# Row blocks of 128 and a remainder, and one transfer per gather, in the expert part of a fused kernel

## The chip, the cores and the metric

One Trainium2 chip; the kernel runs on one core, in one launch. Its engines are TensorE (PE: matmuls, and beside it PEld, the loading of the stationary operand), VectorE (DVE), ScalarE (ACT), GpSimd (POOL) and SyncE (SP, which here only issues transfers). Sixteen DMA engines move data between DRAM and the on-chip memory. The metric is the device time of a launch in microseconds; smaller is better. All data are 4 bytes wide.

## The reference, cut to what matters

A linear-attention recurrence, a dense layer pair, and a layer of eight experts of which every token uses one. The change touches only the last:

```python
N, D, E, F = (3072, 384, 8, 1024)
...
logits = x @ w_gate
e_idx = np.argmax(logits, axis=1)
...
gate_w = probs[np.arange(N), e_idx]
eom = 1.0 / (1.0 + np.exp(-(x @ w_output_gate)))
out = np.zeros((N, D), dtype=np.float32)
for e in range(E):
    mask = e_idx == e
    ...
    h = np.maximum(x[mask] @ w1[e], 0.0)
    ye = h @ w2[e]
    out[mask] = gate_w[mask, None] * eom[mask, e, None] * ye
```

So each token's row of 384 numbers goes through two matrices of one expert, is scaled, and is written to the token's place.

## The kernel before, in words

The first 560 us are attention and the dense pair, for eight blocks of 384 tokens. As each block is done, the rows of its tokens are scattered into a DRAM table `rows`, sorted by expert: a row has 386 numbers (384 values, the scale, the token's number), 1544 bytes. Each expert has its own region of the table, of which the first 512 rows (`CAPS[0]`) are filled beforehand with blank rows whose token number is invalid.

Then come the experts, the fullest first. The list `CAPS` says how many rows each place in that order gets: 512, 456, 432, 424, 408, 384, 384, 372. They are worked as nine segments, numbered 0 to 8: the first expert is two segments of 256 rows, every other one is a segment of its own, so that segment 2 has 456 rows and segment 8, the last, has 372. `segs` holds, for each, the expert, the first row, the number of rows and a tuple with the rows of its token blocks (lines 773 to 777):

```python
mb = -(-n // 128)
segs.append((i, 0, n, (128,) * 3 + (n - 384,) if 384 < n <= 448 else (n // mb,) * mb))
```

That makes 4 blocks of 114 for segment 2, three blocks of 128 and one of 48, 40 or 24 for segments 3 to 5, three of 128 for segments 6 and 7, and three of 124 for segment 8.

For one segment the work is:

- `gather` (L792): SP issues a transfer of the segment's rows from `rows` to the tile `xs`, with a block's rows on as many partitions (L805); where the last block is shorter, a second transfer fetches it (L807).
- `turn_x` (L810): for each of three column groups `kc`, PE transposes the blocks (L815), ACT copies the result to `xe` (L816), DVE forms the low part (L817) and, once, the token numbers `ids` (L820, and L822 for a shorter last block).
- `first` (L830): for each of eight column groups `f`, nine matmuls with all the segment's rows as the moving operand (L839), then ACT and DVE make `hh`.
- `second` (L851): for each block and each `f`, matmuls with the block's columns of `hh` as the stationary operand and 384 columns moving (L867): three for each block, or two where a short last block has both parts of its rows side by side (`packed`, L789).
- `finish` (L870): the blocks are scaled by ACT or DVE (L883, L881, L879), and for each POOL issues an indirect transfer that scatters its rows to `out` (L885).

In this part of the program the order on every engine is that of the code. In segment q, at step f = 2, SP gets the gather of segment q + 1; at f = 4, 5 and 6 PE gets its transposes. Beside that, at steps set by `plan`, SP fetches the next expert's weights in seven pieces (`fetch`, L749 and L754, 512 and 384 KB each) into a few buffers, and ACT with DVE or POOL splits them (`split`, L768, L769). SP works its list in order, so a gather stands behind the fetches before it and ahead of those after it.

At the end, the last three `f` of segment 8 are worked block by block, so that each block's scatter can start while the next is still being multiplied.

Of the kernel before, what the change touches and what calls it, by code (L numbers as in the profile page):

```python
# [18 lines left out]
B, H, S, D = 4, 8, 768, 48  # L19
DM = H * D  # L20
FF = 2048
NT = B * S
E = 8
FE = 1024
CH = 64
TB = 384
NC = TB // CH
NBLK = NT // TB
NP = H // 2
# [20 lines left out]
def consts():  # L50
    c = np.zeros((128, 384), np.float32)
    p = np.arange(128)
    c[:, 0:128] = np.eye(128)
    c[:, 128:192] = (p[:, None] % CH) <= np.arange(CH)[None, :]
    c[:, 192:320] = p[:, None] < p[None, :]
    c[:, 320:328] = E - np.arange(E)
    c[:, 328:336] = np.arange(E)
    c[:, 360:368] = CAPS
    c[:, 368:376] = NT * (p[:, None] < np.arange(E)[None, :])
    c[:, 336:360] = np.arange(NT // 128)[None, :] * 128 + p[:, None]  # L60
    return c
# [3 lines left out]
def tile_kernel(ctx, tc, aps, outs):  # L65
    nc = tc.nc
    pe, act, dve, pool, sp = nc.tensor, nc.scalar, nc.vector, nc.gpsimd, nc.sync
# [23 lines left out]
    rows = dp.tile([E * NT, ROW], F32, name="rows")  # L91
# [358 lines left out]
    sent = {}  # L450

    def apart(key, i):
        # every token has its own row
        for b in sent.setdefault(key, []):
            tc.declare_no_dep(i.ins, b.ins, reason="no two tokens share a row")
        sent[key].append(i)

    def route_send(j):
        oh, ps = rs.pop(j)
        r = rt.pop(j)[0]  # L460
        pr = rp.tile([128, NA, E], F32, name="pr2")
        si = rp.tile([128, NA], I32, name="si")
        dve.tensor_tensor(out=pr, in0=ps[:, 0:NA * E].rearrange("p (a e) -> p a e", e=E), in1=oh, op=ALU.mult)
        with nc.allow_low_precision(reason="whole numbers below 2**24"):
            dve.tensor_reduce(out=si, in_=pr, axis=AX.X, op=ALU.add)
        for a in range(NA):
            apart("rows", pool.indirect_dma_start(
                out=rows, out_offset=bass.IndirectOffsetOnAxis(ap=si[:, a:a + 1], axis=0),
                in_=r[:, a], in_offset=None, bounds_check=E * NT - 1, oob_is_err=False))
        for a in range(NA):  # L470
            dve.tensor_tensor(out=cum, in0=cum, in1=oh[:, a], op=ALU.add)
# [21 lines left out]
    ex = {}  # L493
# [233 lines left out]
    for j in range(NBLK):  # L727
        last = j == NBLK - 1
# [4 lines left out]
        if last:  # L733
# [34 lines left out]
                act.copy(hi, t)  # L768
                (dve, pool)[i % 2].tensor_tensor(out=lo, in0=t, in1=hi.bitcast(F32), op=ALU.subtract)  # L769

            # segments: expert place, first row, rows, rows of its token blocks;
            # a last block of up to 64 rows has both parts of its rows side by side in one stationary operand
            segs = [(0, 0, EARLY, (128,) * 2), (0, EARLY, CAPS[0] - EARLY, (128,) * 2)]
            for i, n in enumerate(CAPS):
                if i:
                    mb = -(-n // 128)
                    segs.append((i, 0, n, (128,) * 3 + (n - 384,) if 384 < n <= 448 else (n // mb,) * mb))
            HH = [mh.tile([128, 2 * CAPS[1]], F32R, name=f"hh{i}") for i in range(3)]
            for t in HH:
                pool.tensor_copy(out=t[:, 384:448], in_=cst[:, 376:377].to_broadcast([128, 64]))  # L780
# [2 lines left out]
            def blocks(q):  # L783
                at = 0
                for m, mr in enumerate(segs[q][3]):
                    yield m, mr, slice(at, at + mr)
                    at += mr

            def packed(q, m):  # L789
                return m == 3 and segs[q][3][3] < segs[q][3][0]  # L790

            def gather(q):  # L792
                e, c0, n, mrs = segs[q]
                mb, mr, full = len(mrs), mrs[0], mrs.count(mrs[0])
                if q == 0:
                    xs = mxe.tile([128, mb, ROW], F32, name="xs0")
                    ids = mxe.tile([128, mb], I32, name="ids0")
                    xe = xp.tile([128, 2, KC, TB], F32R, tag="xT", name="xe0")
                else:
                    xs = mx.tile([128, 4, ROW], F32, tag="xs", name="xs")  # L800
                    ids = mx.tile([128, 4], I32, tag="ids", name="ids")
                    xe = mx.tile([128, 2, KC, CAPS[1]], F32R, tag="xe", name="xe")
                xs, ids, xe = xs[0:mr, 0:mb], ids[0:mr, 0:mb], xe[:, :, :, 0:n]
                rg = rows.rearrange("(e n) c -> e n c", e=E)[bass.ds(ex[e], 1), c0:c0 + n]
                sp.dma_start(out=xs[:, 0:full], in_=rg[:, 0:full * mr].rearrange("e (m p) c -> p (e m) c", p=mr))  # L805
                if full < mb:
                    sp.dma_start(out=xs[0:mrs[full], full], in_=rg[:, full * mr:n].rearrange("e n c -> (e n) c"))  # L807
                ein[q] = xs, ids, xe

            def turn_x(q, kc):  # L810
                n = segs[q][2]
                xs, ids, xe = ein[q]
                ps = tr().tile([128, 512], F32, tag="at", name="pst")
                for m, mr, c in blocks(q):
                    pe.transpose(ps[:, c], xs[0:mr, m, kc * 128:(kc + 1) * 128], ident[0:mr, 0:mr])  # L815
                act.copy(xe[:, 0, kc], ps[:, 0:n])  # L816
                dve.tensor_tensor(out=xe[:, 1, kc], in0=ps[:, 0:n], in1=xe[:, 0, kc].bitcast(F32), op=ALU.subtract)  # L817
                if kc == 0:
                    full = segs[q][3].count(segs[q][3][0])
                    dve.tensor_copy(ids[:, 0:full], xs[:, 0:full, DM + 1])  # L820
                    for m, mr, _ in list(blocks(q))[full:]:
                        dve.tensor_copy(ids[0:mr, m:m + 1], xs[0:mr, m, DM + 1:DM + 2])  # L822

            def lows(q):
                n = segs[q][2]
                if len(segs[q][3]) == 4 and packed(q, 3):
                    return [(slice(0, 384), 512), (slice(384, n), 448)]
                return [(slice(0, n), CAPS[1])]
# [63 lines left out]
        for f in range(NF):  # L892
# [40 lines left out]
            if j == 1 and f < E:  # L933
                sp.dma_start(out=rows[f * NT:f * NT + CAPS[0]].rearrange("(n p) c -> p n c", p=128),
                             in_=blank.unsqueeze(1).to_broadcast([128, CAPS[0] // 128, ROW]))
# [37 lines left out]
    def settle():  # L973
# [17 lines left out]
        pso = moe.enter_context(tc.tile_pool(name="pso", bufs=1, space=PSUM))  # L991
        tr = lambda: pst
    gather(1)
    NS = len(segs)
    plan = {}
# [18 lines left out]
    for q in range(NS):  # L1014
        e = segs[q][0]
# [36 lines left out]
def layout(inputs):  # L1052
    q, k, v, al = (np.asarray(inputs[n]) for n in ("q", "k", "v", "alpha"))
    f4 = np.float32

    def flat(x):
        return np.ascontiguousarray(x).reshape(B * H, S, D)

    raw = np.zeros((NBLK, NP, 128, RAW), f4)
    vnat = np.zeros((NBLK, NP, 128, NA, 2, D), f4)  # L1060
    vw = np.zeros((NBLK, NP, 128, NC, D), f4)

    def put(x, hh):
        # [B,H,S,D] -> [NBLK, NP, D, TB]
        x = x.reshape(B, NP, 2, 2, TB, D)[:, :, hh]
        return x.transpose(0, 2, 1, 4, 3).reshape(NBLK, NP, D, TB)

    apad = np.ones((NBLK, NP, 128, NC, CH), f4)
    for hh in range(2):
        rows = slice(64 * hh, 64 * hh + D)  # L1070
        raw[:, :, rows, 0:TB] = put(k, hh)
        raw[:, :, rows, TB:2 * TB] = put(q, hh)
        apad[:, :, rows] = put(al, hh).reshape(NBLK, NP, D, NC, CH)
        vt = v.reshape(B, NP, 2, 2, TB, D)[:, :, hh].transpose(0, 2, 1, 3, 4).reshape(NBLK, NP, TB, D)
        vc = vt.reshape(NBLK, NP, NC, CH, D).transpose(0, 1, 3, 2, 4)
        vw[:, :, 64 - 64 * hh:128 - 64 * hh] = vc
        vn = vt.reshape(NBLK, NP, NA, 128, D).transpose(0, 1, 3, 2, 4)
        vnat[:, :, :, :, hh] = vn
    wi = np.asarray(inputs["moe_w_in"]).reshape(KC, 128, NF, 128).transpose(2, 1, 0, 3).reshape(NF, 128, 1, DM)
    wo = np.asarray(inputs["moe_w_out"]).reshape(NF, 128, 1, DM)  # L1080
    wio = np.ascontiguousarray(np.concatenate([wi, wo], axis=2))
    if wio.dtype == np.float64:
        wio = wio.view(np.int64)
    a0 = 2 * TB
    raw[:, :, :, a0:a0 + AW - 1].reshape(NBLK, NP, 128, NC, CH + 1)[..., 1:] = apad
    return {
        "cst": consts(), "raw": raw,
        "q": flat(q), "k": flat(k), "v": flat(v), "alpha": flat(al),
        "vn": vnat.reshape(NBLK, NP, 128, NA, 2 * D),
        "vw": vw.reshape(NBLK, NP, 128, NC * D),  # L1090
        "wio": wio,
        "w_gate": np.ascontiguousarray(inputs["moe2_w_gate"]),
        "w_ogate": np.ascontiguousarray(inputs["moe2_w_output_gate"]),
        "w1": np.ascontiguousarray(inputs["moe2_w1"]),
        "w2": np.ascontiguousarray(inputs["moe2_w2"]),
    }
# [14 lines left out]
```

## Time and profile before

| what | value |
|---|---|
| median of 3 runs | 861.94 us (861.24 to 862.06) |
| span of the profiled execution | 857.1 us |
| median less that span | 4.8 us |
| PE busy | 802.5 us, 94% of the span |
| expert part (segments 0 to 8) | about 600 us to the end |
| DMA | 97.94 MB, mean 114 GB/s |

The profile is of one execution and gives its span; what lies around the span isn't in it. In the slices, PE is busy nine tenths or more from the tenth slice on but for one slice near the end, and its granted clock (PEclk) is full but for the beginning and the end. A row of the trace gives the start and length in microseconds, the engine, the line, the operation with what it writes and reads, the count, and in brackets how long the engine had been idle and what ended that.

### The profile page before, as it was taken

To read this page: it belongs to the slowest core of one execution; us is meant where nothing else is said; L and a number is where in the kernel's file an instruction comes from. 1 tells how busy PE (TensorE), PEld (TensorE's weight loads), DVE (VectorE), ACT (ScalarE), POOL (GpSimd) and SP (SyncE) were. 2 spreads that over 40 slices of the span, in tenths; PEclk is the share of its full clock that TensorE was granted. 3 is DMA by queue.
4 is the path that set the end of the run, shared out by engine and by line. 5 is a ranking of instruction groups with operands and counts; after the bars stand their busy time and mean duration, and the time that the engine had idled before them with its cause. 6 is when DMAs were issued, how large, how long until landed. Compare 5 with 4: busy or idle time off the path is not lost. (4 is left out here: it accounts for less than half of the span.)

```text
span 857.1 us, 15706 instructions
## 1 busy us (share of the span) xinstructions
PE 802.5 (94%) x5968; PEld 747.5 (87%) x5968; DVE 520.0 (61%) x1054; ACT 386.2 (45%) x795; POOL 247.1 (29%) x216
## 2 busy tenths in 40 slices
PE   6787878999999999999999999999999999999795
PEld 4566767989989999998999999999999999999794
DVE  8999999666656666666676664455543443444221
ACT  4545445545544544544445544345443343445221
POOL 6367776021210211111121020021332423442221
PEclk9679789999999999999999999999999999999998
DMA  8666542763322232232242220033434425424501
GB/s 252 169 192 182 173 141 92 234 211 88 91 63 81 70 96 76 62 115 63 57 132 57 60 74 15 15 121 124 162 114 164 150 78 188 171 95 147 143 26 29
DMA packets 59968, 97.94 MB, mean 114 GB/s; under 512 B 20290, under 2 KB 46372, under 8 KB 59885
## 3 DMA queue, kind: packets, MB, share of 16 engines
q1 hardware_dynamic: 55932, 87.39, 34.1%
q0 software_dynamic: 3952, 9.47, 3.0%
q8 instruction: 49, 0.80, 0.4%
q14 instruction: 35, 0.28, 0.1%
HBM read 71.60 MB, written 16.25 MB: 102 GB/s over the span
## 5 line engine op out<-in xcount | busy, mean ns | idle before, releaser
L351 PE MATMUL psh<-xT,whi 128*128 128x384 f32 x768 | 209.5, 346 | 15.0 <-DVE t L359 13.0
L373 PE MATMUL x<-gg,ohi 128*128 128x384 f32 x768 | 216.2, 349 | 6.9 <-POOL gg L362 3.6
L351 PEld LDWEIGHTS psh<-xT,whi 128*128 128x128 f32 x768 | 139.6, 192 | 17.9 <-issue 7.0
L373 PEld LDWEIGHTS x<-gg,ohi 128*128 128x128 f32 x768 | 138.2, 190 | 15.9 <-POOL gg L362 4.2
L351 PE MATMUL psh<-xT,wlo 128*128 128x384 f32 x384 | 132.0, 344 | 0.0
L373 PE MATMUL x<-gg,olo 128*128 128x384 f32 x384 | 129.6, 337 | 0.0
L359 DVE TENSOR_TENSOR t<-psh,t 128x384 f32<-128x384 f32 x128 | 70.4, 550 | 75.8 <-ACT t L357 75.0
L867 PE MATMUL o<-hi,hh 128*128 128x384 f32 (+2 forms) x440 | 115.1, 338 | 0.0
L839 PE MATMUL psf<-xe,hi 128*128 128x256 f32 (+6 forms) x432 | 110.4, 340 | 0.0
L361 ACT CAST gg<-t 128x384 fp32r<-128x384 f32 x128 | 65.6, 513 | 73.1 <-DVE t L359 72.1
L357 ACT ACTIVATE t<-psh 128x384 f32<-128x384 f32 x128 | 62.1, 485 | 78.0 <-PE psh L351 77.7
L845 DVE SCALAR_TENSOR_TENSOR hh<-psf,hh 128x384 fp32r<-128x384 f32 (+3 forms) x96 | 40.9, 446 | 91.3 <-ACT hh L843 91.1
L362 DVE TENSOR_TENSOR gg<-t,gg 128x384 fp32r<-128x384 f32 x114 | 63.5, 557 | 36.4 <-ACT gg L361 36.0
L196 POOL TENSOR_TENSOR XB<-raw,P 48x384 f32<-48x384 f32 x32 | 34.8, 1087 | 172.4 <-issue 140.1
L867 PEld LDWEIGHTS o<-hi,hh 128*128 128x128 f32 (+2 forms) x440 | 78.4, 185 | 1.1 <-DVE hh L845 0.3
L839 PEld LDWEIGHTS psf<-xe,hi 128*128 128x128 f32 x432 | 76.6, 190 | 2.6 <-issue 0.3
L769 POOL TENSOR_TENSOR lo<-s,hi 128x768 fp32r<-128x768 f32 (+1 forms) x24 | 48.9, 2037 | 100.5 <-ACT hi L768 99.7
L867 PE MATMUL o<-lo,hh 128*128 128x384 f32 (+2 forms) x232 | 77.7, 337 | 0.0
L843 ACT ACTIVATE hh<-psf 128x256 fp32r<-128x256 f32 (+6 forms) x72 | 34.8, 484 | 94.1 <-PE psf L839 76.2
L351 PEld LDWEIGHTS psh<-xT,wlo 128*128 128x128 f32 x384 | 73.7, 192 | 1.1 <-POOL wlo L333 0.7
L373 PEld LDWEIGHTS x<-gg,olo 128*128 128x128 f32 x384 | 72.5, 189 | 0.1
L839 PE MATMUL psf<-xe,lo 128*128 128x256 f32 (+6 forms) x216 | 72.4, 335 | 0.0
(145 smaller groups left out, 1289.8 us busy)
## 6 DMA issues: line engine op xcount, KB each, us to landing
raw<-raw SPq DMA_DIRECT2D x32, 579.5 KB, 4.6
wst<-wio SPq DMA_DIRECT2D x32, 384.0 KB, 3.6
s<-w SPq DMA_DIRECT2D x24, 512.0 KB, 4.1
s<-w SPq DMA_DIRECT2D x32, 384.0 KB, 6.4
xT<-y SPq DMA_DIRECT2D x48, 144.0 KB, 3.0
rows<-blank SPq DMA_DIRECT2D x8, 772.0 KB, 6.2
VZ<-vn SPq DMA_DIRECT2D x60, 72.0 KB, 2.4
xs<-rows SPq DMA_DIRECT2D x5, 579.0 KB, 7.1
```

The source lines that it names most:

```text
L196: pool.tensor_tensor(out=c3(XB[u % 2])[64:64 + D], in0=c3(q)[64:64 + D], in1=Pc[64:64 + D, :, 1:CH + 1], op=ALU.mult)
L351: pe.matmul(begun[f][:, 0:TB], w[:, kc, fs], xT[j][:, x, kc], start=(kc + n == 0), stop=(kc == KC - 1 and n == 2))
L357: act.activation(out=t, in_=ps[:, 0:TB], func=AF.Tanh)
L359: dve.tensor_tensor(out=g, in0=ps[:, 0:TB], in1=t, op=ALU.subtract)
L361: act.copy(gg[:, 0], g)
L362: (pool if j == 0 and f not in GLD else dve).tensor_tensor(out=gg[:, 1], in0=g, in1=gg[:, 0].bitcast(F32), op=ALU.subtract)
L373: pe.matmul(px[j][k][:, 0:TB], w[:, f, k * 128:(k + 1) * 128], gg[:, gi], start=(f == 0 and n == 0), stop=(f == NF - 1 and n == 2))
L769: (dve, pool)[i % 2].tensor_tensor(out=lo, in0=t, in1=hi.bitcast(F32), op=ALU.subtract)
L839: pe.matmul(ps[:, 0:n], w[:, kc, fs], xe[:, x, kc], start=(i == 0), stop=(i == 3 * KC - 1))
L843: act.activation(out=hh[:, 0:n], in_=ps[:, 0:n], func=AF.Relu)
L845: dve.scalar_tensor_tensor(out=hh[:, o:o + c.stop - c.start], in0=ps[:, c], scalar=0.0, in1=hh[:, c].bitcast(F32), op0=ALU.max, op1=ALU.su ...
L867: pe.matmul(po[q][m][0:p.stop - p.start, 0:DM], hh[:, p], w[:, f], start=(f == 0 and i == 0), stop=(f == NFE - 1 and i == len(parts) - 1))
```

## The change

Three edits. The blocks of every segment are now as many of 128 rows as there are, and a remainder: segment 2 has (128, 128, 128, 72) and segment 8 has (128, 128, 116); the others stay. `packed` is written as a condition on the remainder (up to 64 rows), with the same outcome for every segment. And each gather is one transfer of whole blocks of 128 rows, so that it reads 512 rows for segments 2 to 5 and 384 for segment 8; rows behind the segment's own are read and not used. The token numbers are taken by one DVE instruction.

```diff
-                    mb = -(-n // 128)
-                    segs.append((i, 0, n, (128,) * 3 + (n - 384,) if 384 < n <= 448 else (n // mb,) * mb))
+                    segs.append((i, 0, n, (128,) * (n // 128) + ((n % 128,) if n % 128 else ())))
...
             def packed(q, m):
-                return m == 3 and segs[q][3][3] < segs[q][3][0]
+                return m == 3 and segs[q][3][3] <= 64
...
-                xs, ids, xe = xs[0:mr, 0:mb], ids[0:mr, 0:mb], xe[:, :, :, 0:n]
-                rg = rows.rearrange("(e n) c -> e n c", e=E)[bass.ds(ex[e], 1), c0:c0 + n]
-                sp.dma_start(out=xs[:, 0:full], in_=rg[:, 0:full * mr].rearrange("e (m p) c -> p (e m) c", p=mr))
-                if full < mb:
-                    sp.dma_start(out=xs[0:mrs[full], full], in_=rg[:, full * mr:n].rearrange("e n c -> (e n) c"))
+                xs, ids, xe = xs[:, 0:mb], ids[:, 0:mb], xe[:, :, :, 0:n]
+
+                rg = rows.rearrange("(e n) c -> e n c", e=E)[bass.ds(ex[e], 1), c0:c0 + 128 * mb]
+                sp.dma_start(out=xs, in_=rg.rearrange("e (m p) c -> p (e m) c", p=128))
...
                 if kc == 0:
-                    full = segs[q][3].count(segs[q][3][0])
-                    dve.tensor_copy(ids[:, 0:full], xs[:, 0:full, DM + 1])
-                    for m, mr, _ in list(blocks(q))[full:]:
-                        dve.tensor_copy(ids[0:mr, m:m + 1], xs[0:mr, m, DM + 1:DM + 2])
+                    dve.tensor_copy(ids, xs[:, :, DM + 1])
```

On SP, the gather of segment 3 (`xs` is the tile it fills, `s_...` are weight pieces) stands between two weight pieces; before:

```order
L754 DMA s_7220<-w 128x2x384
L805 ISA
L805 DMA xs<-rows 128x3x386
L807 ISA
L807 DMA xs<-rows 48x386
L754 ISA
L754 DMA s_7253<-w 128x2x384
```

and now:

```order
L754 DMA s_7220<-w 128x2x384
L805 ISA
L805 DMA xs<-rows 128x4x386
L754 ISA
L754 DMA s_7252<-w 128x2x384
```

Two transfers became one of four blocks; segments 4 and 5 read alike. On SP, the gather of segment 8, before:

```order
L749 DMA s_8520<-w 128x1024
L754 ISA
L754 DMA s_8548<-w 128x2x384
L805 ISA
L805 DMA xs<-rows 124x3x386
L754 ISA
L754 DMA s_8577<-w 128x2x384
```

and now:

```order
L749 DMA s_8514<-w 128x1024
L754 ISA
L754 DMA s_8542<-w 128x2x384
L805 ISA
L805 DMA xs<-rows 128x3x386
L754 ISA
L754 DMA s_8571<-w 128x2x384
```

It stands in the same place; only its shape is another. On PE, the first transposes of segment 8 (`pst` is their result, `cst` holds the identity), behind the last `second` matmul of a step of segment 7, before:

```order
L867 MATMUL o_8536<-hi_8277,hh_6049 128x384 x2
L867 MATMUL o_8536<-lo_8278,hh_6049 128x384
L815 MATMUL pst<-cst,xs 128x124 x3
L839 MATMUL psf<-xe,hi_8275 128x384 x2
L839 MATMUL psf<-xe,lo_8276 128x384
```

and now:

```order
L862 MATMUL o_8530<-hi_8271,hh_6049 128x384 x2
L862 MATMUL o_8530<-lo_8272,hh_6049 128x384
L813 MATMUL pst<-cst,xs 128x128 x2
L813 MATMUL pst<-cst,xs 128x116
L834 MATMUL psf<-xe,hi_8269 128x384 x2
L834 MATMUL psf<-xe,lo_8270 128x384
```

The three transposes keep their place and number; the lines have moved up by five. Ahead of the expert part the order of no engine differs.

## Rows read from the trace of the kernel before

**Rows 1.** Page, parts 1 and 2: busy us, share; tenths in 40 slices.

```profile
PE 802.5 (94%) x5968; PEld 747.5 (87%) x5968; DVE 520.0 (61%) x1054; ACT 386.2 (45%) x795; POOL 247.1 (29%) x216
...
PE   6787878999999999999999999999999999999795
```

**Rows 2.** Waits of PE, 590 to 858 us: total us, times, longest.

```profile
PE pst L815 <- SPq L1048: 5.1, 1, 5.1
```

**Rows 3.** Timeline of PE around segment 8's transposes: start us, length us.

```profile
802.45 0.33 PE L867 MATMUL o<-lo,hh 128*128 128x384 f32 x1
807.85 0.85 PE L815 MATMUL pst<-cst,xs 124*128 124x124 f32 x3 [5.06 <-SPq L1048]
...
811.33 0.52 PE L867 MATMUL o<-hi,hh 128*128 128x384 f32 x2
...
812.74 0.34 PE L867 MATMUL o<-lo,hh 128*128 128x384 f32 x1
812.92 0.48 PE L815 MATMUL pst<-cst,xs 124*128 124x124 f32 x3
...
814.82 0.52 PE L867 MATMUL o<-hi,hh 128*128 128x384 f32 x2
```

**Rows 4.** Windows: PE, PEld, DVE, ACT, POOL busy, then PEclk, DMA share, GB/s.

```profile
804.00:808.00 4.00, 0.15 (x1) 0.19 (x2) 0.00 (x0) 0.00 (x0) 0.00 (x0) 0.98 0.29 88
808.00:811.00 3.00, 3.00 (x11) 3.00 (x11) 1.58 (x3) 1.20 (x2) 0.00 (x0) 0.50 0.20 69
```

**Rows 5.** Timeline of SP: the gathers of segments 8, 7, 5, 4, 3.

```profile
794.53 0.29 SPq L805 DMA_DIRECT2D xs<-rows  x1
...
768.27 0.38 SPq L805 DMA_DIRECT2D xs<-rows  x1
...
707.31 0.38 SPq L805 DMA_DIRECT2D xs<-rows  x1
...
675.23 0.38 SPq L805 DMA_DIRECT2D xs<-rows  x1
...
641.16 0.38 SPq L805 DMA_DIRECT2D xs<-rows  x1
```

**Rows 6.** Timeline of PE: first transposes of segments 7, 5, 4, 3.

```profile
776.44 0.49 PE L815 MATMUL pst<-cst,xs 128*128 128x128 f32 x3
...
717.50 0.66 PE L815 MATMUL pst<-cst,xs 128*128 128x128 f32 x4
...
685.96 0.67 PE L815 MATMUL pst<-cst,xs 128*128 128x128 f32 x4
...
653.31 0.68 PE L815 MATMUL pst<-cst,xs 128*128 128x128 f32 x4
```

**Rows 7.** DMA issues from 675 to 675.7 us: KB, us to landing.

```profile
xs<-rows SPq DMA_DIRECT2D x1, 579.0 KB, 7.1
```

**Rows 8.** Timeline of POOL: scatters of segments 7 and 8.

```profile
822.99 0.99 POOL L885 DMA_INDIRECT out<-o,ids  x1 [6.43 <-ACT o L883]
...
844.41 1.33 POOL L885 DMA_INDIRECT out<-o,ids  x1 [17.87 <-ACT o L883]
...
847.67 1.31 POOL L885 DMA_INDIRECT out<-o,ids  x1 [0.30 <-issue]
```

**Rows 9.** DMA issues of scatters in windows from 824.2, 844, 847.5 us.

```profile
out<-o,ids POOLq DMA_INDIRECT x1, 2.5
...
out<-o,ids POOLq DMA_INDIRECT x1, 5.7
...
out<-o,ids POOLq DMA_INDIRECT x1, 6.3
```

**Rows 10.** Groups of PE, 640 to 858 us, by form: busy us, mean ns.

```profile
L867 PE MATMUL o<-hi,hh 128*128 128x384 f32 x240 | 61.5, 337 | 0.0
L867 PE MATMUL o<-hi,hh 128*114 128x384 f32 x62 | 15.9, 337 | 0.0
```

**Rows 11.** The remainder's token numbers on DVE: ns least, median, most.

```profile
L822 DVE CAST ids<-xs x3: 133/138/138, 655.2 to 719.3; 48x1 int32<-48x1 f32 x1, 40x1 int32<-40x1 f32 x1, 24x1 int32<-24x1 f32 x1
```

More of the change, by code (lines that the diff above doesn't have):

```diff
@@ L789, in packed @@
             def packed(q, m):
-                return m == 3 and segs[q][3][3] < segs[q][3][0]
+                return m == 3 and segs[q][3][3] <= 64
             def gather(q):
                 e, c0, n, mrs = segs[q]
-                mb, mr, full = len(mrs), mrs[0], mrs.count(mrs[0])
+                mb = len(mrs)
                 if q == 0:
```

## The prediction

> **What bounds the kernel now.** I read four views in this order. The page's busy shares and slices say who sets the time: PE is busy 94% of the span and nine tenths or more in nearly every slice of the expert part, DVE 61%, ACT 45% and POOL 29% [rows 1]. So what counts is PE's instructions, the holes between them, the clock they run at, and what comes after the last of them. The waits of PE from 590 us on, where the change acts, have one that is long: 5.1 us, once, before the transposes of line 815 [rows 2]. The timeline of PE shows where: the last matmul of a step starts at 802.45, and the first transposes of segment 8 only at 807.85; they are blocks of 124 [rows 3]. The row names an SP instruction of line 1048, which is the end of the program; such a name says only that SP's last event came before. The transposes read the identity, there from the start, and `xs`, so what they wait for is the gather of segment 8. SP issues it at 794.53 [rows 5]: it has not landed 13.3 us later, while the 128-partition gather whose landing is recorded, of 579 KB, took 7.1 us [rows 7].
>
> The windows say why it is slow: from 804 to 808 the DMA engines' mean busy share is 0.29 [rows 4], that is 0.29 x 16 = 4.6 engines' worth of work, while PE waits. A transfer spread over all 16 would have shown a share near 1 and been done. I take it that rows of 124 partitions go out over few engines. From 808 to 811 the granted clock is 0.50, the lower of its two levels (1.2 GHz), after PE has stood idle for 5.06 us [rows 3, 4]; that is a second price of the same wait.
>
> On which engines the rows go: the Trainium skill, "DMA: Bandwidth & Descriptors", section "Why a DMA increments its semaphore by 16 and not by 1", says that the number of engines is the largest up to 16 that divides the slowest dimension of the access pattern; 124 gives 4, and 128 gives 16. The share of 0.29 agrees with 4 engines and a little other traffic [rows 4]. By the same rule the remainder of 116 rows, being 4 x 29, would stay on 4 engines in its scatter, which speaks against a full gain in the tail.
>
> **The gather of segment 8.** It becomes 384 rows on 128 partitions, at the same place in SP's list. What does it take? From below, nothing less than the 2.5 us of the fastest transfer shown [rows 9] need be asked, since early landing is worth nothing. From above, 13.3 us, if the shape does nothing. The nearest row has the same shape and size: 7.1 us [rows 7]. Its sister for segment 7, issued at 768.27 in the same place of its segment, was there for the transposes at 776.44, 8.17 us later, with no wait before them [rows 5, 6]. I take 7.1: landed at 794.53 + 7.1 = 801.63. In a step without a wait the transposes start 812.92 - 812.74 = 0.18 us after the start of the last matmul [rows 3], so PE wants the rows at 802.45 + 0.18 = 802.63. The gather is 1.0 us early.
>
> What goes, then: from 802.63 to the first `second` matmul after the transposes a step without a wait takes 814.82 - 812.92 = 1.90 us, so that matmul starts at 804.53 and not at 811.33 [rows 3]. That is 6.8 us: 5.2 of waiting (807.85 - 802.63) and 1.6 of half clock (811.33 - 807.85 - 1.90). What is late next: ACT, DVE and POOL follow PE here and have idle time, DVE at 61% the least [rows 1]; the weight pieces behind the gather in SP's list land sooner too, as they no longer stand behind it on its engines. The wait in [rows 2] is PE's only one over 1 us from 590 us on, so I find nothing else of this size. All 6.8 us lie on the path to the end, as PE runs without a hole from there.
>
> **The tail.** The scatters of the last segment now have 128, 128 and 116 rows in place of three times 124. Scatters of 128 rows take POOL 0.99 us and land after 2.5; those of 124 take 1.33 and land after 5.7 when alone; the last, issued at 847.67 behind two others, lands after 6.3, at 853.97, 3.1 us before the end [rows 8, 9]. With the first two out of the way in 2.5 us each, the last stands alone. Its price lies between 2.5 (as 128 rows) and 6.3 us (as now); the nearest row is the lone 124: 5.7 x 116 / 124 = 5.3. So 1.0 us is saved if the end follows that landing, nothing if something else holds it, and at most 3.8. More than now I exclude: it has fewer rows and less ahead of it. I take 1.0.
>
> **What costs nothing.** The second matmuls of segment 2 go from 114 columns of stationary operand to 128 and 72: 337 ns on average in either form [rows 10], and their number stays. The transposes keep their number: three of 124 take 0.48 us, three of 128 take 0.49 [rows 3, 6]. Segments 3 to 5 each lose one transfer's issue on SP and one DVE instruction of about 138 ns [rows 11]; nobody on the path waits for either. The blocks of segment 2 scatter and gather in another shape, where PE has no wait now.
>
> **What it adds.** 56 + 80 + 88 + 104 rows more are read for segments 2 to 5 and 12 for segment 8: 340 rows of 1544 bytes, 0.5 MB of 98. Their gathers may land later. Scaled from 7.1 us for 384 rows, 512 rows take at most 9.5. The time they have is from issue to first transposes: 653.31 - 641.16 = 12.2 us for segment 3, 685.96 - 675.23 = 10.7 for segment 4, 717.50 - 707.31 = 10.2 for segment 5 [rows 5, 6]. So they are in time by 0.7 us or more. Without that cover each would cost its lateness in idle PE, and up to 1.6 us of half clock.
>
> **The sum.** 6.8 + 1.0 = 7.8 us off a span of 857.1, so 849.3. The median of the runs lies 861.94 - 857.1 = 4.8 us above the span; nothing in the change touches what lies there, so 854.1 us.
>
> **The rivals.**
> 1. The gather is spread, but lands late all the same, since the weight pieces around it take the engines too. For it: only one landing of this shape is recorded, and weight pieces stand on both sides of the gather in SP's list. Against it: the sister of segment 7 met its 8.2 us with no wait. Price: if it took the 9.5 us that I grant to 512 rows, it would land at 804.0, 1.4 us late, with a half clock of 1.6 at worst: 854.1 + 3.0 = 857.1.
> 2. The last scatter lands like one of 128 rows, after 2.5 us: 2.8 us more are won: 851.3. For it: if more than the number of partitions decides, a lone scatter is fast. Against it: the lone scatter of 124 took 5.7 [rows 9].
> 3. The change doesn't do what it says at the place that counts: PE waits at 802.6 for something other than the gather, such as the event that the row names. Then only the tail is left: between 861.9 and 860.9. Against it: the operands of the transposes leave nothing else.
> 4. Slower: a gather's time goes by its rows, whatever the partitions. 13.3 us for 372 rows is 35.8 ns a row, so 384 rows take 13.7 and 512 take 18.3. Then segments 3, 4 and 5 come late by 6.1, 7.6 and 8.1 us at their first transposes, with 1.6 of half clock each, and segment 8 by 0.4 more: 27 us, so 889. It decides from a landing of more than 10.2 us for 512 rows. Against it: 384 rows landed in 7.1 us [rows 7].
>
> **How the numbers follow.** My forecast of 854.1 gets 0.77; its own range is 852.8 (the clock and the step of before, with a scatter 1.3 us better) to 855.5 (no gain in the tail, and 0.4 us of spread between runs). Rival 1 gets 0.08, rival 2 0.08, rival 3 0.04 and rival 4 0.03. For 8 in 10 I reach up to rival 1 and most of the way down to rival 2: 851.6 to 857.1. About 0.2%, 1.7 us, is what a measurement of this kernel can tell from no change. The forecast and rivals 1 and 2 are faster by more: 0.93. Rival 3 is within it: 0.04. Rival 4 is slower: 0.03.
>
> **What would show it.** Right: in the profile of the changed kernel the transposes of segment 8 start within 0.3 us of the matmul before them, the granted clock stays full from there to the last matmul, and the stretch after the transposes that took 8.9 us (802.45 to 811.33) takes 2.1. The first two of the last three scatters take POOL 1.0 us and land after 2.5; the last still takes 1.3 and lands after about 5.3. Wrong: a wait of PE before the transposes of any segment, segment 5 first, or the old wait at segment 8. If the wait is gone and the time has still not fallen by 6 us, a new hole lies after 804 us, and my claim that nothing else is late is what failed.

## The result, and the profile after

The changed kernel takes 853.3 us (median of 4 runs, 852.4 to 855.5) where the kernel before takes 862.0 (4 runs, 861.2 to 863.9): a ratio of 0.991, with a 95% interval of 0.989 to 0.993. The forecast was 854.1. A second set on another occasion gave 0.990 (0.987 to 0.992).

The waits of PE from 590 us on have lost their first line; the longest left is the one of 0.7 us, which was there before as well (columns as in [rows 2]):

```profile
PE pst L813 <- DVE xe L815: 0.7, 1, 0.7
```

The timeline of PE around segment 8's first transposes shows no hole, where [rows 3] has one of 5.06 us:

```profile
803.89 0.34 PE L862 MATMUL o<-lo,hh 128*128 128x384 f32 x1
804.07 0.48 PE L813 MATMUL pst<-cst,xs 128*128 128x128 f32 x3
...
805.97 0.51 PE L862 MATMUL o<-hi,hh 128*128 128x384 f32 x2
...
807.55 0.48 PE L813 MATMUL pst<-cst,xs 128*128 128x128 f32 x3
```

The transposes follow 0.18 us after the start of the matmul before them, and the next `second` matmul comes 2.08 us after that start; in [rows 3] it came 8.88 us after. The difference is 6.80 us. In the windows (columns as in [rows 4]) PE is busy throughout and the granted clock is full, where it was at its lower level from 808 to 811:

```profile
804.00:808.00 4.00, 4.00 (x27) 3.93 (x26) 2.05 (x4) 1.70 (x3) 0.00 (x0) 1.00 0.30 99
808.00:811.00 3.00, 3.00 (x19) 3.00 (x18) 1.10 (x2) 1.70 (x3) 1.65 (x1) 1.00 0.01 3
```

The gather itself, in the timeline of SP and in a window:

```profile
795.66 0.37 SPq L805 DMA_DIRECT2D xs<-rows  x1
...
799.00:800.00 1.00, 1.00 (x7) 1.00 (x7) 0.29 (x1) 1.00 (x2) 0.00 (x0) 1.00 1.05 392
```

In the trace its rows are packets of 1544 bytes. They run from 798.6 to 801.22, and 213 of the 384 end between 799 and 800, when all 16 DMA engines are busy (share 1.05: the recorded times of packets overlap a little).

The end, in the timeline: the last matmul, and the three scatters of segment 8 on POOL, two of which before are in [rows 8]:

```profile
840.99 0.34 PE L862 MATMUL o<-lo,hh 128*116 128x384 f32 x1
...
839.05 0.97 POOL L880 DMA_INDIRECT out<-o,ids  x1 [17.86 <-ACT o L878]
840.67 0.97 POOL L880 DMA_INDIRECT out<-o,ids  x1 [0.65 <-DVE o L876]
842.25 1.27 POOL L880 DMA_INDIRECT out<-o,ids  x1 [0.61 <-ACT o L878]
```

The two of 128 rows take POOL 0.97 us and no longer 1.33; the one of 116 takes 1.27. The landings of these three are not recorded in this profile, but the windows show when the DMA engines fall silent (share in the last column but one):

```profile
847.00:847.50 0.50, 0.00 (x0) 0.00 (x0) 0.00 (x0) 0.00 (x0) 0.00 (x0) 0.50 0.03 12
847.50:848.00 0.50, 0.00 (x0) 0.00 (x0) 0.00 (x0) 0.00 (x0) 0.00 (x0) 0.50 0.00 0
```

That is at most 5.3 us after POOL took it. From the start of the last matmul to the end of the span are 850.6 - 841.0 = 9.6 us, and before they were 857.1 - 846.3 = 10.8.

**Measuring from a mark near the change.** The medians say 8.7 us, the ratio 8.0, the spans 6.5. Which? The first transposes of segment 7 stand at 776.44 before [rows 6], and here at

```profile
777.88 0.49 PE L813 MATMUL pst<-cst,xs 128*128 128x128 f32 x3
```

1.4 us later, with the same program ahead of them on every engine but for the gathers and segment 2's blocks, and segments 2 to 6 without a wait in both. Over all thirteen traces of this study that point lies between 775.75 and 779.16. So the first nine tenths of the program vary by 3.4 us from one execution to the next, nearly half the effect, and I compare from there to the end of the span. That stretch is 857.1 - 776.4 = 80.7 us before and 850.6 - 777.9 = 72.7 now: 7.9 less with all digits, where the sum said 7.8. Spans are given to 0.1 us, so the last column below holds to about 0.1.

| kernel | span | segment 7's transposes | from there to the end |
|---|---|---|---|
| before | 857.1 | 776.44 | 80.7 |
| changed | 850.6 | 777.88 | 72.7 |
| changed, again (`e10`) | 851.9 | 779.16 | 72.7 |
| `e1`, before, gather on 112 + 12 | 852.9 | 778.57 | 74.3 |
| `e2`, changed, segment 8 as before | 858.6 | 777.18 | 81.4 |
| `e3`, before, 384 rows | 849.0 | 777.71 | 71.3 |
| `e4`, changed, 384 rows | 847.3 | 776.02 | 71.3 |
| `e11`, the same again | 848.8 | 777.74 | 71.1 |
| `e5`, gather on 124 + 4 | 858.2 | 777.33 | 80.9 |
| `e6`, gather on 126 + 2 | 848.4 | 775.75 | 72.7 |
| `e7`, gather on 122 + 6 | 860.7 | 776.90 | 83.8 |
| `e8`, gather on 125 + 3 | 853.6 | 776.23 | 77.4 |
| `e9`, gather in two pieces | 850.7 | 777.97 | 72.7 |

### The profile page after: what moved, and what is told of

The parts are those of the page before. It is cut to its first block, busy times and chain, and to the rows that moved or that the text cites. A ratio compares the mean times of both kernels' runs of the same rounds, so it can differ in the third digit from the quotient of the medians.

```text
span 850.6 us, 15695 instructions
## 1 busy us (share of the span) xinstructions
PE 799.6 (94%) x5968; PEld 743.8 (87%) x5968; DVE 517.1 (61%) x1051; ACT 385.6 (45%) x795; POOL 247.2 (29%) x216
## 4 chain that ended last, share of the span: by engine, by line
PE 56%; DVE 19%; issue 8%; DMA 8%; ACT 5%; SPq 2%; POOL 2%; another core or an unknown queue 0%; POOLq 0%; DVEq 0%; ACTq 0%
PE x L373 13%; PE psh L351 12%; PE o L862 11%; PE psf L834 11%; DMA raw<-raw 6%; DVE t L359 2%; DVE Ex L174 2%; PE psg L422 2%; DVE w L308 2%; DVE w L310 2%; PE psu L252 2%; DVE XA L195 2%; DVE SS L256 2%; DVE gg L362 2%; PE pss L221 1%
## 5 line engine op out<-in xcount | busy, mean ns | idle before, releaser
L862 PE MATMUL o<-lo,hh 128*128 128x384 f32 (+1 forms) x232 | 77.7, 337 | 0.0
L373 PEld LDWEIGHTS x<-gg,olo 128*128 128x128 f32 x384 | 72.7, 189 | 0.1
```

The source lines that it names most:

```text
L373: pe.matmul(px[j][k][:, 0:TB], w[:, f, k * 128:(k + 1) * 128], gg[:, gi], start=(f == 0 and n == 0), stop=(f == NF - 1 and n == 2))
L862: pe.matmul(po[q][m][0:p.stop - p.start, 0:DM], hh[:, p], w[:, f], start=(f == 0 and i == 0), stop=(f == NFE - 1 and i == len(parts) - 1))
```

## The experiments

My theory: the time of a gather goes by how many engines its partitions divide over; nothing else in the change matters but that and the same thing in the last scatters. The rivals: the blocks of 128 in the computation, or the whole-block reads, brought it.

**1. Only the transfer's partitions, in the kernel before.**

```diff
-sp.dma_start(out=xs[:, 0:full], in_=rg[:, 0:full * mr].rearrange("e (m p) c -> p (e m) c", p=mr))
+src = rg[:, 0:full * mr].rearrange("e (m p) c -> p (e m) c", p=mr)
+for p0, p1 in ((0, 112), (112, 124)) if mr == 124 else ((0, mr),):
+    sp.dma_start(out=xs[p0:p1, 0:full], in_=src[p0:p1])
```

> The kernel before, with one edit: segment 8's gather goes out as two transfers, of partitions 0 to 111 and of 112 to 123. Blocks of 124, matmuls and scatters stay. My theory (the shape of the transfer decides on how many engines its rows go): both parts land within about 7 us, the 5.1 us wait of PE before segment 8's transposes and the half clock behind it go, the tail stays: 6.8 us less than before, about 855.2. Rival (the gain came with the blocks of 128 in compute and scatter, or with the whole-block reads of other segments): no change, about 862, wait still there.

Measured: 0.993 of before (0.991 to 0.995), 854.2 us where before had 860.0. The timeline of PE and the last scatter on POOL:

```profile
804.58 0.34 PE L869 MATMUL o<-lo,hh 128*128 128x384 f32 x1
804.75 0.48 PE L817 MATMUL pst<-cst,xs 124*128 124x124 f32 x3
...
843.03 1.31 POOL L887 DMA_INDIRECT out<-o,ids  x1 [0.30 <-issue]
```

The blocks are still of 124, the rows and bytes are the same, and the wait is gone. The scatter costs POOL what it did. The stretch to the end is 74.3: 6.4 less than before and 1.6 more than the changed kernel. The wait and the half clock gave the expected 6.8; the tail, from the start of the last matmul to the end of the span, took 11.2 us where it took 10.8 before, with the same scatters. The 1.6 to the changed kernel (tail 9.6) is what blocks of 128 bring in the tail, by these two traces.

**2. The change without segment 8.** In the changed kernel:

```diff
-segs.append((i, 0, n, (128,) * (n // 128) + ((n % 128,) if n % 128 else ())))
+segs.append((i, 0, n, (124,) * 3 if n == 372 else (128,) * (n // 128) + ((n % 128,) if n % 128 else ())))
...
-rg = rows.rearrange("(e n) c -> e n c", e=E)[bass.ds(ex[e], 1), c0:c0 + 128 * mb]
-sp.dma_start(out=xs, in_=rg.rearrange("e (m p) c -> p (e m) c", p=128))
+rg = rows.rearrange("(e n) c -> e n c", e=E)[bass.ds(ex[e], 1), c0:c0 + mr * mb]
+sp.dma_start(out=xs, in_=rg.rearrange("e (m p) c -> p (e m) c", p=mr))
```

> The changed kernel, with segment 8 put back to three blocks of 124 gathered on 124 partitions; segments 2 to 5 keep the change's blocks and single transfers of 512 rows. My theory: everything that was won lies in segment 8, so the wait of 5 us, the half clock and the slow scatters are back: 861.5 to 862. Rival (the single transfers or segment 2's blocks bring a part): below 860.

Measured: 1.0005 of before (0.9989 to 1.002), 860.2 us against 860.0. The timeline of PE has the hole again:

```profile
803.19 0.33 PE L862 MATMUL o<-lo,hh 128*128 128x384 f32 x1
808.43 0.85 PE L813 MATMUL pst<-cst,xs 124*128 124x124 f32 x3 [4.91 <-SPq L1043]
...
814.68 0.48 PE L813 MATMUL pst<-cst,xs 124*128 124x124 f32 x3
```

So segment 2's new blocks and the single transfers of 512 rows for segments 2 to 5 are worth nothing that can be measured, and cost nothing, within 0.2%.

**3. The number of engines, as a dose.** Four kernels, one run each: the changed kernel with segment 8's gather cut at partition 124, 126, 122 or 125, everything else the same. For 124:

```diff
-sp.dma_start(out=xs, in_=rg.rearrange("e (m p) c -> p (e m) c", p=128))
+src = rg.rearrange("e (m p) c -> p (e m) c", p=128)
+for p0, p1 in ((0, 124), (124, 128)) if n == 372 else ((0, 128),):
+    sp.dma_start(out=xs[p0:p1], in_=src[p0:p1])
```

> The changed kernel, but segment 8's gather of 384 rows goes out as partitions 0 to 123 and 124 to 127. My theory (the largest number up to 16 that divides the partitions is the number of engines: 4 here, 93 rows on each): lands about 13 us after issue, PE waits about 5 us before segment 8's transposes and runs at half clock after it: 6.8 us over the changed kernel. Rival (blocks of 124 in compute, not the transfer, made the wait): no wait.

> The changed kernel, but segment 8's gather goes out as partitions 0 to 125 and 126 to 127. My theory: 126 is 14 x 9, so 14 engines with 27 rows each and no wait of PE: the changed kernel's time. Rival (a transfer of anything but 128 partitions is slow): a wait of about 5 us as with 124.

> The changed kernel, but segment 8's gather goes out as partitions 0 to 121 and 122 to 127. My theory: 122 is 2 x 61, so 2 engines with 183 rows each, about twice the rows of the case of 124: lands some 20 to 25 us after issue, PE waits 12 to 17 us, with half clock behind. Rival (only the number of rows, or being off 128, counts): like the case of 124, a wait of about 5 us.

> The changed kernel, but segment 8's gather goes out as partitions 0 to 124 and 125 to 127. My theory: 125 is 5 x 25, so 5 engines with 75 rows each: at 0.1 us a row and 3 us before the first it lands after about 11 us, PE waits about 3 us. It also shows whether the clock falls after a wait of that length; I expect that it does, with some 1.5 us lost. Rival: a wait as long as with 124.

Measured: 860.0 us for 124, 850.2 for 126, 862.4 for 122 and 855.4 for 125, where the kernel before had 862.3 in a single run. The first transposes of segment 8 in the timeline of PE, for 124, 122 and 125 with the wait in brackets and the next transposes behind it, and for 126 without a wait:

```profile
809.15 0.86 PE L815 MATMUL pst<-cst,xs 128*128 128x128 f32 x3 [5.48 <-SPq L1045]
...
815.13 0.48 PE L815 MATMUL pst<-cst,xs 128*128 128x128 f32 x3
```

```profile
812.60 0.85 PE L815 MATMUL pst<-cst,xs 128*128 128x128 f32 x3 [9.36 <-SPq L1045]
...
817.52 0.48 PE L815 MATMUL pst<-cst,xs 128*128 128x128 f32 x3
```

```profile
805.56 0.53 PE L815 MATMUL pst<-cst,xs 128*128 128x128 f32 x3 [2.98 <-DMA xs<-rows]
...
810.61 0.48 PE L815 MATMUL pst<-cst,xs 128*128 128x128 f32 x3
```

```profile
801.94 0.48 PE L815 MATMUL pst<-cst,xs 128*128 128x128 f32 x3
```

Here the computation has blocks of 128 in all four, and the bytes are the same. With 126 partitions (14 x 9) PE doesn't wait; with 125 (5 x 25) it waits 3.0 us, with 124 (4 x 31) 5.5, with 122 (2 x 61) 9.4. The order is that of the largest divisor up to 16. Among these four it is also that of the distance from 128; what speaks against the distance is that 112 + 12, farther off than any of them, was free too. In the 125 case the trace names the transfer itself as what PE waited for, and settles what the event of an SP instruction in [rows 2] stood for. The divisor is the rule of the Trainium skill, "DMA: Bandwidth & Descriptors", section "Why a DMA increments its semaphore by 16 and not by 1"; these waits agree with it. No view names the engines that a transfer used, but the DMA share counts them. Here are stretches in which SP's queue moves nothing but packets of 1544 bytes, rows of the gather, for 122, 125 and 124 (columns as in [rows 4]):

```profile
799.00:802.00 3.00, 3.00 (x19) 3.00 (x18) 1.25 (x2) 1.08 (x3) 1.84 (x1) 1.00 0.13 50
```

```profile
801.00:802.00 1.00, 1.00 (x8) 1.00 (x7) 0.42 (x1) 0.49 (x1) 0.07 (x1) 1.00 0.31 96
```

```profile
805.00:807.00 2.00, 0.00 (x0) 0.00 (x0) 0.00 (x0) 0.00 (x0) 0.00 (x0) 1.00 0.28 78
```

Of 16 engines these shares are 2.1, 5.0 and 4.5, close to the 2, 5 and 4 of the divisor. For 124 I had expected 6.8 us over the changed kernel. The stretches to the end differ by 8.2 (80.9 and 72.7), as the half clock cost more than before. For 125 the wait of 3 us and the 1.5 of half clock came out as 3.0 and 1.6.

My numbers for 122 were wrong: I expected 12 to 17 us of waiting, from twice the rows on each engine at the same time a row. From issue (794.66) to the transposes it took 17.9 us for 183 rows an engine by the rule, against 809.15 - 795.09 = 14.1 us for 93. Time a row isn't fixed. A reason can be seen on SP, in the issues of the two transfers (ns, least, median and most of two), for 122, 124, 125 and 126:

```profile
L807 SPq DMA_DIRECT2D xs<-rows x2: 321/3691/7061, 794.7 to 795.2; - x2
```

```profile
L807 SPq DMA_DIRECT2D xs<-rows x2: 338/1262/2187, 795.1 to 795.6; - x2
```

```profile
L807 SPq DMA_DIRECT2D xs<-rows x2: 346/749/1152, 794.0 to 794.6; - x2
```

```profile
L807 SPq DMA_DIRECT2D xs<-rows x2: 243/324/404, 793.5 to 794.1; - x2
```

The first transfer is issued in 0.32 to 0.40 us. The second, of a few partitions, keeps SP for 7.06, 2.19, 1.15 and 0.24 us (for 126 the second is the shorter one), as if SP could not hand it over while the engines of the first were full; that reason is an inference, no view shows it. In the case of 122 the weight pieces behind it go out only from 802.5 us on, and until then the gather has its engines to itself. The packets bear out that this matters: 33 rows end per us from 799 to 802, with no weight piece under way, and 23 from 804 to 808, beside weight pieces.

**4. The old gather with the new blocks.** The changed kernel, with the gather put back:

```diff
-sp.dma_start(out=xs, in_=rg.rearrange("e (m p) c -> p (e m) c", p=128))
+sp.dma_start(out=xs[:, 0:full], in_=rg[:, 0:full * mr].rearrange("e (m p) c -> p (e m) c", p=mr))
+if full < mb:
+    sp.dma_start(out=xs[0:mrs[full], full], in_=rg[:, full * mr:n].rearrange("e n c -> (e n) c"))
...
```

> The changed kernel's blocks with the old gather: the full blocks in one transfer on 128 partitions, the remainder (72, 48, 40, 24, and 116 rows for segment 8) in a second of its own rows only, and its token numbers in a DVE instruction of their own. My theory: 116 is 4 x 29, so segment 8's second transfer has 29 rows on each of 4 engines and lands within about 7 us of the first issue; PE doesn't wait and the time is the changed kernel's within 0.3%. So the whole-block reads would be worth nothing beside the new division. Rival (reading whole blocks in one transfer is what removed the wait): a wait of PE before segment 8's transposes and 5 us or more over the changed kernel.

Measured: 0.991 (0.988 to 0.993), the changed kernel beside it 0.990 (0.987 to 0.992); both stretches to the end are 72.7. SP's issues and the transposes:

```profile
795.75 0.38 SPq L805 DMA_DIRECT2D xs<-rows  x1
796.34 0.29 SPq L807 DMA_DIRECT2D xs<-rows  x1
...
804.15 0.48 PE L815 MATMUL pst<-cst,xs 128*128 128x128 f32 x3
```

No wait, although the remainder of 116 rows goes out as 4 x 29: a third of the rows is quick enough here even on few engines (4 by the rule). Reading whole blocks in one transfer makes the code simpler; the time came from the division.

**5. One number instead.** `CAPS` ends in 384 and not 372, once in the kernel before (whose old rule then gives three blocks of 128) and twice in the changed one.

```diff
-CAPS = (512, 456, 432, 424, 408, 384, 384, 372)
+CAPS = (512, 456, 432, 424, 408, 384, 384, 384)
```

> The kernel before with one number changed: the last expert gets 384 rows and not 372, so that its old rule gives three blocks of 128. My theory: wait and half clock go (6.8 us), the last scatter lands after 2.5 us as every one of 128 rows and not 6.3 (3.8 us), and 72 matmuls of 384 columns for 372 cost 0.4 us: 862.0 - 10.2 = 851.8, below the changed kernel's 853.3. Rival (the new division and single transfers are needed): not below 853.3.

> The changed kernel with 384 rows for the last expert. My theory: only the tail moves against the changed kernel: the last scatter lands after 2.5 us and not 5.3, 72 matmuls cost 0.4 us more: 853.3 - 2.4 = 850.9, within 1 us of the kernel before with 384 rows. Rival (something else than the last landing holds the end): 853.3 to 853.7.

> The changed kernel itself, once more, so that the others of this call stand beside it on one chip: about 0.991 of the kernel before, 6.8 us from the wait and 1.0 from the tail.

> The changed kernel with 384 rows for the last expert, on the same chip as the changed kernel: the last scatter lands after 3.6 us of its issue by SP's wait and not 5.3, 72 matmuls cost about 0.35 us more, so 1.3 to 2.5 us below the changed kernel. Rival: no difference, the first run's gain was the chip's.

Measured: 0.988 (0.986 to 0.990) for the kernel before with 384 rows and 0.989 (0.987 to 0.991) for the changed one; on the other occasion 0.989 (0.986 to 0.991), with the changed kernel at 0.990 beside it. By the ratios alone 384 rows can't be told from the changed kernel, as the intervals overlap. The stretch to the end tells them apart: 71.3, 71.3 and 71.1 us against 72.7 twice, 1.4 to 1.6 less. For the kernel before I had expected 10.2 us from the change to 384 rows, and the stretch shows 9.4. The 1.4 is also less than the 2.4 I expected of the second, though the last is within its 1.3 to 2.5. In the trace of the changed kernel with 384 rows, the last scatter on POOL and the windows after it:

```profile
840.70 0.97 POOL L880 DMA_INDIRECT out<-o,ids  x1 [0.56 <-ACT o L878]
...
842.00:844.00 2.00, 0.00 (x0) 0.00 (x0) 0.00 (x0) 0.00 (x0) 0.00 (x0) 1.00 0.24 84
844.00:845.00 1.00, 0.00 (x0) 0.00 (x0) 0.00 (x0) 0.00 (x0) 0.00 (x0) 0.55 0.00 0
```

The 128 rows are out within 3.3 us, sooner than 116 took (5.3). So with more rows and more columns the kernel is faster, and the whole change is matched by one digit group in a list. By the stretch to the end, the two with 384 rows are the fastest of the versions run.

## Why the prediction was right, point by point

- **The wait is the gather's, and the shape makes it slow.** Shown. `e1` takes it away by the partitions of the transfer alone, `e5` brings it back the same way (both send two transfers, so their number isn't the cause), and the waits and DMA shares of `e5` to `e8` follow the divisor. The share near 1 that I supposed for a transfer over all engines is there in the changed kernel (1.05). One reading was inexact: I wrote that the gather had not landed 13.3 us after its issue, but that is when the transposes start; its last row's packet ends at 807.24, 12.7 us after the issue.
- **Landing in time.** The step took 7.1 us and left 1.0 to spare. It held: there is no wait in five traces with 128 partitions at that place, and in the changed kernel the last row's packet ends 5.6 us after the issue (801.22 - 795.66). The landing itself isn't recorded. In the five traces where PE waited for the gather, its transposes started 0.6 to 1.1 us after the last such packet; taken from there, the gather landed after an estimated 6.2 to 6.7 us, some 2 us before PE wanted it at 804.07. Rival 1 did not happen.
- **6.8 us for the wait and the half clock.** 6.80 in the changed kernel's timeline, from the same two marks. The step held, but its smaller part, the half clock, is luckier than it looks. From one group of transposes to the next a step at full clock takes 807.55 - 804.07 = 3.48 us. Before, it took 5.07 (812.92 - 807.85 in [rows 3]), 1.6 more, and that is what I removed. In `e2` it took 814.68 - 808.43 = 6.25, 2.8 more, and in `e5` 815.13 - 809.15 = 5.98, 2.5 more, after waits of about the same length as before. So the clock's share is 1.6 in one execution and up to 2.8 in another, and the 1.6 that rival 1 takes for the worst is no upper bound. In `e2` the granted clock is at its lower level until 814.5, where before it was back at 811.3:

  ```profile
  809.00:814.00 5.00, 5.00 (x18) 5.00 (x17) 2.13 (x4) 1.69 (x3) 0.00 (x0) 0.50 0.08 28
  ```

  The 81.4 us in `e2` instead of 80.7 are these 1.2 us more, less 0.2 of a shorter wait and 0.3 of a shorter tail.
- **The tail, 1.0 us.** 1.1 by the traces (10.8 to 9.6 us with all digits), and 1.6 between `e1` and the changed kernel. The tails of the three traces with scatters of 124 rows are 10.8, 11.2 (`e1`) and 10.5 us (`e2`), so the gain lies between 0.9 and 1.6, and 7.8 meeting 7.9 to a tenth is in part luck. That the end follows the last landing, which I had left open, is shown by `e3` and `e4`: a quicker landing, an earlier end.
- **Rival 2's price was too high.** I had a scatter of 128 rows at 2.5 us from one in the middle of the program. That row is not the rule for 128 rows even before: the third scatter of segment 3, issued at 705.08, landed after 5.6. At the end the 128 rows of `e4` are followed by traffic for up to 3.3. Since that rival's condition (a fast scatter of 116) didn't come about, this cost the forecast nothing, but the 2.8 us there, and the 2.4 in the expectation of `e4`, should have been some 1.5 to 2.
- **Costs nothing, adds nothing.** `e2`: 1.0005. Rival 4 is out with it: 512 rows in one transfer make no segment wait.
- **What I mis-sized is the base.** I took 4.8 us between the span and the median for time outside the span, and added it to the new span. It is mostly spread between executions: the changed kernel's run of 852.43 us has a span of 850.6, so 1.8 lie outside. The profiled execution before was a quick one; the kernel before has been seen from 858.6 to 865.4 us in all. The forecast of a difference doesn't suffer by it, since the same was added on both sides, but the forecast's own range should have carried 3 us of spread and not 0.4.

## What to carry to other kernels

When a transfer is slow, look at its outermost dimension before its bytes: with 384 rows on 128 partitions this gather was in time, with 372 rows on 124 it was not, and with the same 372 rows cut at 112 it was again. A size that is cut to the work's exact need (372 rows) can cost more than a round one with some waste (384), as it decides the shape of every transfer made from it. And where an effect of 1% sits at the end of a long program, measure from a mark shortly ahead of it in each trace: here that cut the spread between executions from 3 us to 0.1 or 0.2 for the kernels without a wait behind the mark (72.7 four times, 71.1 to 71.3 three times).

## What the runs showed of the hardware

- SP is held up behind a gather of badly divided partitions: issuing the next piece of it took 7.06 us after 122 partitions, 2.19 after 124, 1.15 after 125 and 0.24 after 126. Behind the 124 partitions of the kernel before, issuing the weight piece took 1.94 us, and behind the 128 of the changed one 0.37. So such a transfer delays the list behind it and not only its own reader.
- The granted clock fell to its lower level (1.2 GHz) in all five traces in which PE waited for the gather, for 3.0, 4.9, 5.1, 5.5 and 9.4 us (`e8`, `e2`, before, `e5`, `e7`), and what that cost does not follow the wait: the step after it was longer than 3.48 us by 1.6, 2.8, 1.6, 2.5 and 1.4. It follows the time that PE then worked at the lower level, which by the trace's record of the clock was 3.4, 6.0, 3.4, 5.4 and 3.0 us: the cost is nearly half of it each time.
- In the last segment the scatters take POOL 0.97 us for 128 rows, 1.27 for 116, and 1.30 to 1.33 for 124. Rows alone don't set it: in the kernel before, the third scatter of segment 3 has 128 rows and takes 1.86. That the divisor governs the scatters too is not shown.

  ```profile
  705.08 1.86 POOL L885 DMA_INDIRECT out<-o,ids  x1 [0.30 <-PE psf L839]
  ```
